# Retention and two feed-forward stages on one core: value weights as the first block row, one product added in PSUM onto a copied bank, and half of the second stage's weights converted during the first

## Chip, cores and metric

The kernel runs on one core of a Trainium2 chip. The metric is device time in microseconds; lower is better. Two figures are used: the time of whole runs (three of the kernel before), and the span of one profiled execution, from its first to its last instruction.

## What is computed

```python
ret = (q @ k.T / sqrt(64)) * Dmat           # causal, Dmat = gamma_h ** (i - j)
x   = (ret @ v), heads side by side         # 2304 tokens x 512
h   = x @ w_in                              # 512 -> 2048
x   = elu(h) @ w_out                        # 2048 -> 512
out = (sigmoid(x @ w_gate) * (x @ w_val)) @ w_o2    # 512 -> 1536 -> 512
```

Inputs are float32; the weights come as pairs of 32-bit words that the kernel converts to float32 itself.

## The kernel before

Every matmul operand is kept as two float32r parts, hi and lo (`split`, lines 105 to 108: ACT casts hi, then POOL or DVE subtracts to get lo), and every product is three matmuls, hi·hi, hi·lo and lo·hi (`mm3`, lines 110 to 114). Every weight tile (128x512) passes through a chain of five stages (`Weight.chain`, lines 137 to 160): stage 1 two ACT instructions (L145, L146), stage 2 two DVE ones (L148, L149), stage 3 one (L152), stage 4 one (L154), stage 5 the split (ACT L107, POOL L108). `load` fetches the raw words by a DMA on SP's queue into one of two buffers.

The order on every engine is the order in which the program is written; nothing reorders it afterwards. The kernel has three parts.

**Retention** (first 125 us): 18 steps, interleaved with pass 0 of the first feed-forward stage.

**First feed-forward stage** (`FF`): 8 passes over d_ff, two blocks `f` of 128 in each; within a pass five token groups `g` (four of 512 tokens, one of 256), so 10 steps per pass. A step makes 12 matmuls up into a bank `h`, ELU (ACT L347, L348, DVE L351), a split into `g`, and two steps later (`LAG`) 12 matmuls down into four `acc` banks; after the second block of a group DVE adds the four banks to `y` (L387). The weights of the next pass, four tiles, are converted in four of the ten steps; `stage()` advances the running chain at four places of a step, and once more at the start of the next.

**Second feed-forward stage**: token groups (0, 1) and then (2, 3) as two `Pair`s, and the last group, 256 tokens, together with pair 0. For the gate and value weights a pair uses Strassen's scheme in Winograd's form: seven half-size `product`s (6 matmuls each) in place of eight, on sums of weights (`Sums`, tile `s`) and on differences of x (`Pair.sum`). There are 12 blocks `f`, each one `unit`: the seven products, sums of them on ACT and DVE, sigmoid and multiplication, splits, and between the products up to five `down`s (6 matmuls each, output tiles of two earlier blocks), placed by `fill(j)`. In pair 0 a unit ends with `single`, 24 matmuls of 256 columns for the last group. In pair 0 `background(f)` converts block f+1's weights `g`, `v`, their sums `s`, and block f's `2`; `bg()` in the unit advances it. The converted tiles are stored to DRAM (`save`) and fetched again for pair 1 (`restore`), both on SP's queue. The first weights of this stage, and the differences of x for pair 0 (`prep`), are made in the last pass of the first stage.

In PSUM the second stage before has four banks that `unit` and `single` take in turn and four for `down`.

Of the kernel before, what the change touches and what calls it, by code (L numbers as in the profile page):

```python
# [47 lines left out]
def retention_elu_glu(  # L48
# [23 lines left out]
    ps_h = ctx.enter_context(tc.tile_pool(name="ps_h", bufs=2, space=bass.MemoryType.PSUM))  # L72

    h_bank = lambda: ps_h.tile([128, 512], F32, tag="h", name="h")

    class Ring:
        def __init__(self, name, pool, n, shape, dtype):
            self.name, self.shape, self.dtype, self.at = name, shape, dtype, 0
            self.homes = [(pool, f"{name}{i}") for i in range(n)]

# [3 lines left out]
        def __call__(self, i=None):  # L84
            if i is None:
                i, self.at = self.at, self.at + 1
            pool, tag = self.homes[i % len(self.homes)]
            return pool.tile(self.shape, self.dtype, tag=tag, name=self.name)
# [4 lines left out]
    w_tile = Ring("w", wpool, 8, [128, 2, DM], F32R)  # L93
    x_tile = lambda g: xpool.tile([128, 2, KB, N[g]], F32R, tag=f"x{g}", name=f"x{g}")
    y_tile = lambda g: ypool.tile([128, KB * N[g]], F32, tag=f"y{g}", name=f"y{g}")

    def u_banks(ps_u):
        at = [0]

        def bank():  # L100
            at[0] += 1
            return h_bank() if at[0] % 2 else ps_u.tile([128, 512], F32, tag="u", name="u")
        return bank
# [25 lines left out]
    class Weight:  # L129
        def __init__(self, src, slot, at=None):  # L130
            self.src, self.slot, self.at, self.w = src, slot, at, None
# [5 lines left out]
        def chain(self, lo_engine=pool):  # L137
# [19 lines left out]
            w = w_tile(self.slot)  # L157
# [6 lines left out]
    for fs in passes:  # L164
        of_pass.append([])
        for f in fs:
            for n, src in (("i", w_in), ("o", w_out)):
                W[n, f] = Weight(src[f], len(weights) % 8)
                weights.append(W[n, f])
                of_pass[-1].append(W[n, f])  # L170


    class Sums:
# [4 lines left out]
        def chain(self):  # L178
            (g0, g1), (v0, v1) = ((t[:, : DM // 2], t[:, DM // 2 :]) for t in (W[n, self.f].f for n in "gv"))
            dve.tensor_tensor(out=v1, in0=v0, in1=v1, op=ALU.add)  # L180
            dve.tensor_tensor(out=v0, in0=g0, in1=v0, op=ALU.subtract)
            yield
            dve.tensor_tensor(out=g0, in0=v1, in1=g0, op=ALU.subtract)
            dve.tensor_tensor(out=g1, in0=g1, in1=g0, op=ALU.subtract)
            yield
            w = s_tile(self.f)
            split(w[:, 0, 0], w[:, 1, 0], W["v", self.f].f, pool)
            split(w[:, 0, 1], w[:, 1, 1], W["g", self.f].f, pool)
            self.w = w
            yield  # L190

    for f in range(FB):
        W["g", f] = Weight(w_gate[f], f % 2 * 3, 0)
        W["v", f] = Weight(w_val[f], f % 2 * 3 + 1, 1)
        W["2", f] = Weight(w_o2[f], (2, 6, 5, 7)[f % 4], 2)
# [196 lines left out]
    class Pair:  # L392
# [23 lines left out]

        def split(self, name, lo_engine):
            p = self.place(name)
            split(p[:, 0], p[:, 1], self.f32(name), lo_engine)
            self.x[name] = p.rearrange("p i (k t) -> p i k t", k=KH)  # L420
# [21 lines left out]
    def unit(pair, f, bg, fill):  # L442

        A, B, D = u_bank(), u_bank(), u_bank()
        s1, s2, s4, sg = (e_tile() for _ in range(4))
        product(1, pair, f, A, True)
        act.copy(s1, A)
        finish_later()
        fill(5)
        bg()  # L450
        product(2, pair, f, B, True)
        dve.tensor_tensor(out=s1, in0=s1, in1=B, op=ALU.add)
        bg()
        fill(0)
# [21 lines left out]
    def glu(g, f, a, b, engine=pool):  # L476
        engine.tensor_tensor(out=a, in0=a, in1=b, op=ALU.mult)  # L477

        def rest():
            n = N[g]  # L480
            if g == 4:
                gt = x_of[3].rearrange("p i k t -> p (i k t)")[:, 2048 + f % 3 * 2 * n : 2048 + (f % 3 + 1) * 2 * n]
                gt = gt.rearrange("p (i t) -> p i t", i=2)
            else:
                gt = g_tile()
            gb[g, f] = gt
            split(gt[:, 0], gt[:, 1], a, pool)
        return rest

    def single(g, f, bg):  # L490
# [3 lines left out]
        hs = []  # L494
        for w in (W["g", f].w, W["v", f].w):
            h = u_bank()[:, :n]
            hs.append(h)
            for k in range(KB):
                c = slice(k * 128, k * 128 + 128)
                mm3(h, w[:, 0, c], w[:, 1, c], x[:, 0, k], x[:, 1, k], k == 0, k == KB - 1)  # L500
            bg()
            if len(hs) == 1:
                act.activation(out=e, in_=h, func=AF.Sigmoid)
        later.append(glu(g, f, e, hs[1], dve))
# [18 lines left out]
    with tc.manual_schedule():  # L523
# [116 lines left out]
        conv = {2: weights[3]}  # L640
        for P in range(len(passes) - 1):
            a, b, ws = begins[P], begins[P + 1], of_pass[P + 1]
            a += 6 * (P == 0) + LAG * (P == 1)
            for i, w in enumerate(ws):
                conv[a + (i * (b - a)) // len(ws)] = w
        a = begins[-2]
# [256 lines left out]
```

## Time and profile before

| | |
|---|---|
| runs | 938.14, 934.47, 936.83 us; median 936.83 us |
| profiled execution | 938.95 us, its span 937.2 us |
| mean granted TensorE clock | 0.987 |
| PE busy | 894.9 us, 95% of the span |
| DVE, ACT, POOL busy | 546.5, 418.2, 408.9 us (58%, 45%, 44%) |

PE's busy time is made of modelled ends: a matmul that follows another at once is shown as overlapping it. What a stretch loses is therefore read from starts of matmuls and their number, and from the waits.

### The profile page before, as it was taken

What the parts mean: (1) busy time and instruction counts of PE and PEld (TensorE: products, weight loads), DVE (VectorE), ACT (ScalarE), POOL (GpSimd) and SP (SyncE); (2) the same over time, 40 slices, a digit from 0 to 9 for tenths busy, and PEclk for the clock granted to TensorE, in tenths of its full rate; (3) what the DMA queues carried; (4) which work ended last, traced back from release to release, by engine and by line L of the source; (5) the groups of instructions that cost most, each with busy time, mean ns of one, the idle gap of its engine ahead of it and who ended that gap; (6) DMA issues with size and microseconds to landing.
All of it is one profiled execution on the core that took longest, in us unless ns stands there. A gap on an engine that the chain in (4) does not pass through costs nothing.

```text
span 937.2 us, 15632 instructions
## 1 busy us (share of the span) xinstructions
PE 894.9 (95%) x6322; PEld 750.1 (80%) x6322; DVE 546.5 (58%) x838; ACT 418.2 (45%) x766; POOL 408.9 (44%) x327
## 2 busy tenths in 40 slices
PE   7899999999999999999988989989999899999997
PEld 5789988888888888888766778777777788888886
DVE  3767635555554645555875878788877732232323
ACT  2345555544545454445554555554544323222221
POOL 1255523333323333333546656665666632323232
PEclk9999999999999999999998999999999999999999
DMA  9646311111111111111034455555455454534232
GB/s 343 204 169 199 98 46 48 66 45 36 33 45 45 45 46 46 46 45 45 23 135 169 169 169 173 200 209 182 171 202 190 157 208 174 202 147 153 105 124 90
DMA packets 43895, 117.18 MB, mean 125 GB/s; under 512 B 8112, under 2 KB 15280, under 8 KB 40752
## 3 DMA queue, kind: packets, MB, share of 16 engines
q1 hardware_dynamic: 42416, 114.70, 35.5%
q10 hardware_dynamic: 1408, 1.49, 0.5%
q8 instruction: 49, 0.80, 0.3%
q14 instruction: 22, 0.18, 0.1%
HBM read 83.15 MB, written 33.03 MB: 124 GB/s over the span
## 4 chain that ended last, share of the span: by engine, by line
PE 67%; DVE 14%; issue 6%; POOL 6%; ACT 5%; DMA 2%; ACTq 0%; POOLq 0%; DVEq 0%; SPq 0%
PE acc L112 10%; PE acc L114 10%; PE acc L113 10%; PE h L113 8%; PE h L112 8%; PE h L114 8%; PE to L241 3%; PE u L112 3%; PE u L113 3%; PE u L114 3%; POOL w L108 2%; DVE t L149 2%; PE h L337 2%; DVE t L152 2%; DVE t L154 2%
## 5 line engine op out<-in xcount | busy, mean ns | idle before, releaser
L108 POOL TENSOR_TENSOR g<-e,g 128x512 fp32r<-128x512 f32 (+1 forms) x134 | 164.4, 1235 | 265.4 <-ACT g L107 209.9
L112 PE MATMUL h<-x,w 128*128 128x512 f32 (+1 forms) x400 | 145.4, 363 | 0.3 <-DVE e L351 0.3
L113 PE MATMUL h<-x,w 128*128 128x512 f32 (+1 forms) x400 | 145.3, 363 | 0.0
L114 PE MATMUL h<-x,w 128*128 128x512 f32 (+1 forms) x400 | 144.8, 362 | 0.0
L351 DVE SCALAR_TENSOR_TENSOR e<-e,h 128x512 f32<-128x512 f32 (+1 forms) x88 | 51.9, 590 | 138.6 <-ACT e L348 138.2
L112 PE MATMUL acc<-g,w 128*128 128x512 f32 (+1 forms) x352 | 124.9, 355 | 4.7 <-DVE y L387 2.4
L477 POOL TENSOR_TENSOR e<-e 128x512 f32<-128x512 f32 x48 | 63.0, 1313 | 142.5 <-ACT e L468 99.9
L114 PE MATMUL acc<-g,w 128*128 128x512 f32 (+1 forms) x352 | 124.6, 354 | 0.3 <-DVE w L108 0.2
L113 PE MATMUL acc<-g,w 128*128 128x512 f32 (+1 forms) x352 | 124.4, 354 | 0.0
L107 ACT CAST g<-e 128x512 fp32r<-128x512 f32 (+1 forms) x136 | 75.3, 571 | 81.2 <-DVE e L351 74.7
L108 POOL TENSOR_TENSOR w<-t,w 128x512 fp32r<-128x512 f32 x65 | 87.6, 1353 | 44.2 <-ACT w L107 44.1
L518 DVE TENSOR_TENSOR y<-y,acc 128x512 f32<-128x512 f32 x90 | 61.0, 684 | 68.4 <-PE acc L114 68.0
L347 ACT ACTIVATE e<-h 128x512 f32<-128x512 f32 (+1 forms) x88 | 45.9, 521 | 115.7 <-PE h L114 101.9
L112 PEld LDWEIGHTS h<-x,w 128*128 128x128 f32 x400 | 75.8, 189 | 13.0 <-DVE e L351 0.7
L113 PEld LDWEIGHTS h<-x,w 128*128 128x128 f32 x400 | 75.7, 189 | 11.9
L114 PEld LDWEIGHTS h<-x,w 128*128 128x128 f32 x400 | 75.6, 189 | 12.0
L387 DVE TENSOR_TENSOR y<-y,acc 128x512 f32<-128x512 f32 (+1 forms) x140 | 79.2, 628 | 0.1
L112 PEld LDWEIGHTS acc<-g,w 128*128 128x128 f32 x352 | 67.0, 190 | 15.0 <-ACT g L107 4.0
L114 PE MATMUL acc<-w,g 128*128 128x512 f32 x192 | 75.7, 394 | 0.8 <-POOL g L108 0.8
L112 PE MATMUL acc<-w,g 128*128 128x512 f32 x192 | 76.0, 396 | 0.0
L113 PE MATMUL acc<-w,g 128*128 128x512 f32 x192 | 76.0, 396 | 0.0
L114 PEld LDWEIGHTS acc<-g,w 128*128 128x128 f32 x352 | 67.1, 190 | 10.1 <-DVE w L108 0.4
(121 smaller groups left out, 1779.8 us busy)
## 6 DMA issues: line engine op xcount, KB each, us to landing
s<-s SPq DMA_DIRECT2D x24, 1024.0 KB, 5.8
in<-in_ain SPq DMA_DIRECT2D x12, 1024.0 KB, 5.7
raw<-in_w_in SPq DMA_DIRECT2D x16, 512.0 KB, 3.5
raw<-in_w_out SPq DMA_DIRECT2D x14, 512.0 KB, 3.5
raw<-in_w_gate SPq DMA_DIRECT2D x12, 512.0 KB, 5.1
raw<-in_w_val SPq DMA_DIRECT2D x12, 512.0 KB, 3.7
raw<-in_w_o SPq DMA_DIRECT2D x12, 512.0 KB, 3.5
g<-w SPq DMA_DIRECT2D x12, 512.0 KB, 5.4
```

The costliest lines, as they stand in the source:

```text
L107: act.copy(hi, src)
L108: lo_engine.tensor_tensor(out=lo, in0=src, in1=hi.bitcast(F32), op=ALU.subtract)
L112: pe.matmul(out_, wh, xh, start=start, stop=False, skip_group_check=shared)
L113: pe.matmul(out_, wh, xl, start=False, stop=False, skip_group_check=shared)
L114: pe.matmul(out_, wl, xh, start=False, stop=stop, skip_group_check=shared)
L149: dve.tensor_scalar(out=u, in0=u, scalar1=5, scalar2=2, op0=ALU.logical_shift_left, op1=ALU.logical_shift_right)
L241: return pe.matmul(out_, w, x, start=start, stop=True, skip_group_check=True)
L347: act.activation(out=e, in_=h, func=AF.Relu, scale=-1.0)
L351: dve.scalar_tensor_tensor(out=e, in0=e, scalar=-1.0, in1=h, op0=ALU.add, op1=ALU.max)
L387: dve.tensor_tensor(out=y[:, e], in0=y[:, e], in1=a, op=ALU.add)
L477: engine.tensor_tensor(out=a, in0=a, in1=b, op=ALU.mult)
L518: dve.tensor_tensor(out=o, in0=o, in1=a, op=ALU.add)
```

## The change

1. **Roles of the weights.** Value weights take the first block row of the Winograd scheme and gate weights the second (`product`: `"vg"` for `"gv"`; `Sums.chain` with g and v exchanged). Value results then come out where the gate results were.
2. **One sum in PSUM.** In `unit` ACT copies the first product, bank A, into a third bank B, where it used to copy it to SBUF; product 2 is added onto B by matmuls that don't start a new sum, so the DVE addition of the two is gone. The order is products 1, 7, 6, 2, 5, 3, 4 (before 1, 2, 7, 6, 5, 3, 4). A single small matmul opens B in the very first unit.
3. **Multiplications.** The sigmoid now works on the two SBUF sums; the two multiplications are on DVE and read the other factor from PSUM (before on POOL, from SBUF).
4. **Banks.** `unit` has five banks in turn, `down` and `single` three; the two halves of `single` share one bank.
5. **Weights of odd blocks** of the second stage (`g`, `v`, `s`, `2` of f = 1, 3, .., 11) are converted in passes 1 to 6 of the first stage, one block in each, into two tiles of the `g` ring that were not used otherwise in that stage (the ring has four tiles there in place of six); they go to DRAM and come back one unit ahead. A pass so converts seven tiles and a `Sums` in eight of its ten steps. In pair 0 `background` has only the even blocks, spread over two units.
6. **Around the border.** `prep` is spread over the last pass one instruction at a time; in that pass only `g`, `v`, `s` of block 0 are converted (before also `g`, `v` of block 1). The two left-over downs of the first stage, the last group's `single` of block 0, and pair 1's differences have other places.

```diff
@@ product, Sums.chain @@
-                w = W["gv"[int(a[0]) - 1], f].w[:, :, at : at + 128]
+                w = W["vg"[int(a[0]) - 1], f].w[:, :, at : at + 128]
@@ unit @@
-        A, B, D = u_bank(), u_bank(), u_bank()
-        s1, s2, s4, sg = (e_tile() for _ in range(4))
+        A, D, B = u_bank(), u_bank(), u_bank()
+        s2, s4 = e_tile(), e_tile()
+        if not u_seen:
+            pe.matmul(B, W["v", f].w[:, 0, :128], pair.x["11"][:, 0, 0], start=True, stop=True, skip_group_check=True)
+        u_seen.append(f)
         product(1, pair, f, A, True)
-        act.copy(s1, A)
+        act.copy(B, A)
         finish_later()
-        fill(5)
+        fill(0)
         bg()
-        product(2, pair, f, B, True)
-        dve.tensor_tensor(out=s1, in0=s1, in1=B, op=ALU.add)
-        bg()
-        fill(0)
         product(7, pair, f, D, True)
         bg()
         product(6, pair, f, A)
         act.copy(s2, A)
-        act.activation(out=s1, in_=s1, func=AF.Sigmoid)
+        fill(1)
         bg()
-        fill(1)
+        product(2, pair, f, B)
+        bg()
         product(5, pair, f, A)
         act.copy(s4, A)
         dve.tensor_tensor(out=s4, in0=s4, in1=D, op=ALU.add)
+        fill(2)
+        act.activation(out=s4, in_=s4, func=AF.Sigmoid)
         bg()
-        fill(2)
         product(3, pair, f, A)
-        act.activation(out=sg, in_=A, func=AF.Sigmoid)
+        dve.tensor_tensor(out=s4, in0=s4, in1=A, op=ALU.mult)
+        bg()
         fill(3)
         product(4, pair, f, D)
-        later.append(glu(pair.g + 1, f, sg, s4))
+        parts(pair.g + 1, f, s4)
         dve.tensor_tensor(out=s2, in0=s2, in1=D, op=ALU.add)
+        bg()
         fill(4)
-        later.append(glu(pair.g, f, s1, s2))
+        act.activation(out=s2, in_=s2, func=AF.Sigmoid)
+        dve.tensor_tensor(out=s2, in0=s2, in1=B, op=ALU.mult)
+        later.append(lambda: parts(pair.g, f, s2))
@@ which step converts what @@
+        for P in range(1, len(passes)):
+            a, f = begins[P], 2 * P - 1
+            if P == len(passes) - 1:
+                items = {0: W["g", 0], 1: W["v", 0], 2: W["s", 0]}
+            else:
+                i0, o0, i1, o1 = of_pass[P + 1]
+                items = {0: i0, 1: W["g", f], 2: o0, 3: W["v", f], 4: W["s", f], 5: i1, 6: W["2", f], 7: o1}
+            for i, w in items.items():
+                conv[a + i + LAG * (P == 1)] = w
@@ prep: one instruction per call of stage() in the last pass @@
+            yield from [()] * (4 * 4)
+            yield from [[i] for i in x("11", pool) + x("21", pool)]
+            yield from [()] * 4
+            yield from [[t("t1")], [t("t3")], *[[i] for i in x("t1", dve)]]
+            h, l = x("t3", pool)
+            yield from [[h], [l, t("t2")], *[[i] for i in x("t2", dve)]]
...
@@ background @@
-            order = "gvgvgvgvgv2s2s2s22" if 0 < f < FB - 1 else "22222" if f else "2s2s2s22"
+            if f % 2 == 0 and f + 2 < FB:
+                names = "gggvgvvv"
...
+            elif f + 1 < FB:
+                names = "2222gvsss2"
@@ loop over units @@
+                    if f and f % 2 == 0:
+                        restore(f + 1, "gvs2")
...
-                at = (1, 2, 3, 4, 2)
+                at = (1, 2, 3, 4, 4) if f else (0, 1, 2, 3, 4)
```

ACT's queue, a whole round of one unit in the middle of pair 0, before: L447, L458, L463 are the copies of bank A after products 1, 6 and 5, L459 and L468 the sigmoids, L503 that of `single`, L107 the casts, L145 and L146 the first stage of a weight's chain.

```order
L503 ACTIVATE e<-h 128x256
L107 CAST w<-t 128x512
L447 COPY e<-h 128x512
L107 CAST g<-e 128x512 x2
L107 CAST x_113<-e 128x256
L145 ACTIVATE t<-raw 128x512
L146 ACTIVATE raw<-raw 128x512
L145 ACTIVATE t<-raw 128x512
L146 ACTIVATE raw<-raw 128x512
L458 COPY e<-h 128x512
L459 ACTIVATE e<-e 128x512
L463 COPY e<-h 128x512
```

The same in the changed kernel, from a unit's first product to its last, odd block: L455 is the copy A to B, L462 and L468 the copies after products 6 and 5, L471 and L482 the sigmoids, L99 the casts, L137 and L138 the first stage of a weight.

```order
L455 COPY u<-u 128x512
L99 CAST g<-e 128x512
L99 CAST x_113<-e 128x256
L137 ACTIVATE t<-raw 128x512
L138 ACTIVATE raw<-raw 128x512
L462 COPY e<-u 128x512
L468 COPY e<-u 128x512
L471 ACTIVATE e<-e 128x512
L99 CAST w<-t 128x512 x2
L99 CAST g<-e 128x512
L482 ACTIVATE e<-e 128x512
```

Between the copy after product 1 and the copy after product 6 there were seven instructions, four of them stage 1 of two weights; now there are five, two of them stage 1 of one weight.

DVE's queue in a pass of the first stage, before: the end of a step with a conversion, a step without one, the start of the next conversion.

```order
L351 SCALAR_TENSOR_TENSOR e<-e,h 128x512
L154 SCALAR_TENSOR_TENSOR t<-raw,t 128x512
L387 TENSOR_TENSOR y_1300<-y_1300,acc 128x512 x4
L351 SCALAR_TENSOR_TENSOR e<-e,h 128x512
L148 TENSOR_SCALAR t<-t 128x512
L149 TENSOR_SCALAR t<-t 128x512
```

The same place in the changed kernel: L140 to L146 are the chain, L348 the ELU, L384 the additions to `y`.

```order
L348 SCALAR_TENSOR_TENSOR e<-e,h 128x512
L146 SCALAR_TENSOR_TENSOR t<-raw,t 128x512
L384 TENSOR_TENSOR y_1300<-y_1300,acc 128x512 x4
L140 TENSOR_SCALAR t<-t 128x512
L141 TENSOR_SCALAR t<-t 128x512
L144 ISA t<-raw,t 128x1024
L348 SCALAR_TENSOR_TENSOR e<-e,h 128x512
L146 SCALAR_TENSOR_TENSOR t<-raw,t 128x512
```

The next conversion now begins right behind the four additions, ahead of the next step's ELU.

## Rows read from the trace of the kernel before

**Rows 1.** Stretches: us, busy us (and instructions) of PE, PEld, DVE, ACT, POOL; clock; DMA.
```profile
476.13:730.23 254.10, 233.13 (x1116) 192.12 (x1117) 198.79 (x281) 132.03 (x239) 157.34 (x115) 0.97 0.51 181
750.00:900.00 150.00, 150.00 (x651) 121.99 (x650) 44.38 (x65) 41.03 (x73) 50.05 (x39) 1.00 0.48 174
122.00:450.00 328.00, 327.65 (x1599) 276.42 (x1600) 177.18 (x301) 164.10 (x293) 113.48 (x95) 1.00 0.14 44
```

**Rows 2.** Matmuls of 256 columns at pair 0's end: start us, us, instruction.
```profile
729.99 0.28 PE L113 MATMUL u<-x,w 128*128 128x256 f32 x1
730.11 0.28 PE L114 MATMUL u<-x,w 128*128 128x256 f32 x1
```

**Rows 3.** PE at the start of pair 1 and near the end, [idle before <-releaser].
```profile
734.14 0.49 PE L112 MATMUL h<-x,s 128*128 128x512 f32 x1 [1.00 <-ACT x L107]
736.72 0.80 PE L113 MATMUL h<-x,s 128*128 128x512 f32 x1 [2.09 <-DVE x L108]
...
923.24 0.49 PE L114 MATMUL acc<-w,g 128*128 128x512 f32 x1 [0.84 <-POOL g L108]
```

**Rows 4.** Whom PE waited for most, 450 to 745 us: total us, times, longest us.
```profile
PE u L112 <- ACT e L458: 9.3, 6, 2.1
PE h L112 <- ACT e L458: 5.4, 4, 1.4
```

**Rows 5.** ACT around one such wait (columns as rows 3).
```profile
628.94 0.67 ACT L145 ACTIVATE t<-raw 128x512 f32<-128x512 f32 x1
...
630.35 0.67 ACT L145 ACTIVATE t<-raw 128x512 f32<-128x512 f32 x1 [0.19 <-DMA raw<-in_w_val]
...
631.67 0.59 ACT L458 COPY e<-u 128x512 f32<-128x512 f32 x1
```

**Rows 6.** PE at the same place: fill's first and last matmul, next product.
```profile
629.35 0.39 PE L112 MATMUL acc<-w,g 128*128 128x512 f32 x1
...
630.49 0.39 PE L114 MATMUL acc<-w,g 128*128 128x512 f32 x1
632.30 0.50 PE L112 MATMUL u<-x,s 128*128 128x512 f32 x1 [1.43 <-ACT e L458]
```

**Rows 7.** One unit of pair 0, from stall to stall (columns as rows 1).
```profile
632.30:653.38 21.08, 19.67 (x96) 16.32 (x97) 17.56 (x26) 10.88 (x21) 13.47 (x11) 1.00 0.54 189
```

**Rows 8.** Pair 1: product 2's first matmul, then ACT's copy of product 1.
```profile
846.06 0.39 PE L112 MATMUL h<-x,w 128*128 128x512 f32 x1
...
846.26 0.59 ACT L447 COPY e<-u 128x512 f32<-128x512 f32 x1 [4.84 <-PE u L114]
```

**Rows 9.** First-stage steps with a conversion: ACT, then DVE (columns as rows 3).
```profile
306.18 0.62 ACT L107 CAST w<-t 128x512 fp32r<-128x512 f32 x1
...
311.01 0.62 ACT L107 CAST g<-e 128x512 fp32r<-128x512 f32 x1 [0.82 <-DVE e L351]
311.54 0.66 ACT L145 ACTIVATE t<-raw 128x512 f32<-128x512 f32 x1
...
304.85 0.69 DVE L351 SCALAR_TENSOR_TENSOR e<-e,h 128x512 f32<-128x512 f32 x1 [1.16 <-ACT e L348]
305.46 0.69 DVE L154 SCALAR_TENSOR_TENSOR t<-raw,t 128x512 uint32<-128x512 uint32 x1
306.06 2.47 DVE L387 TENSOR_TENSOR y<-y,acc 128x512 f32<-128x512 f32 x4
...
312.23 1.07 DVE L148 TENSOR_SCALAR t<-t 128x512 f32<-128x512 f32 x1 [1.25 <-ACT t L145]
...
313.88 0.69 DVE L152 CUSTOM_DVE_ANT_0 t<-raw,t 128x1024 uint16<-128x1024 uint16 x1
```

**Rows 10.** PE: first matmul of the next downs after that evacuation.
```profile
308.67 0.40 PE L112 MATMUL acc<-g,w 128*128 128x512 f32 x1
```

**Rows 11.** L149 on DVE, 125:450 us, then 560:717: busy us, mean ns | idle.
```profile
L149 DVE TENSOR_SCALAR t<-t 128x512 uint32<-128x512 uint32 x26 | 11.1, 427 | 0.9
...
L149 DVE TENSOR_SCALAR t<-t 128x512 uint32<-128x512 uint32 x21 | 23.2, 1103 | 0.7
```

More of the change, by code (lines that the diff above doesn't have):

```diff
@@ L638, in retention_elu_glu @@
                 begins.append(len(ff))
[L640 to L646, printed above, removed]
-        conv.update({a: W["g", 0], a + 2: W["v", 0], a + 4: W["s", 0], a + 6: W["g", 1], a + 8: W["v", 1]})
-        loads = {}
-        for s, w in conv.items():
-            if w not in weights[:4] and isinstance(w, Weight):
-                loads.setdefault(max(0, s - 2), []).append(w)
@@ new lines, in retention_elu_glu, with convert @@
+        raw_order = [conv[s] for s in sorted(conv) if isinstance(conv[s], Weight)]
+        for f in range(0, FB, 2):
+            raw_order += [W[n, f + 2] for n in "gv" if f + 2 < FB] + [W["2", f]]
+        loads = {}
+        for s in range(NSTEP):
+            if s in conv and conv[s] in of_pass[1]:
+                loads.setdefault(s - 2, []).append(conv[s])
+        done = []
+        copies = {}
+        def convert(w, name=None):
+            i = raw_order.index(w) if isinstance(w, Weight) else len(raw_order)
+            for n, _ in enumerate(w.chain()):
+                if n == 3 and 3 <= i < len(raw_order) - 2:
+                    raw_order[i + 2].load()
+                if name and n == (2 if name[0] == "s" else 4):
+                    done.append(name)
+                yield
@@ new lines, in save, with restore @@
+        def save():
+            while done:
+                n, f = done.pop(0)
+                w = W[n, f].w
+                copies[n, f] = dpool.tile(list(w.shape), F32, tag=f"{n}{f}", name=f"{n}{f}")
+                sp.dma_start(out=copies[n, f], in_=w.bitcast(F32))
+        def restore(f, names):
+            for n in names:
+                w = W[n, f].w = s_tile(f % 2) if n == "s" else w_tile(SLOT[n](f))
+                sp.dma_start(out=w.bitcast(F32), in_=copies[n, f])
+        name_of = {id(w): n for n, w in W.items() if n[0] in "gv2s"}
@@ L668, in retention_elu_glu, with ready @@
+        def ready():
+            for work in prep():
+                for i in work:
+                    i()
+                yield
+        halves, prepared = None, ready()
         end = len(ff)
@@ L721, in retention_elu_glu @@
-        done = []
-        def background(f):
-            order = "gvgvgvgvgv2s2s2s22" if 0 < f < FB - 1 else "22222" if f else "2s2s2s22"
-            chains = {n: W[n, f + (n != "2")].chain() for n in set(order)}
-            seen = {n: 0 for n in chains}
-            for n in order:
-                next(chains[n])
-                seen[n] += 1
-                if n != "s" and seen[n] == 4:
-                    at = raws_of.index((n, f + (n != "2"))) + 2
-                    if at < len(raws_of):
-                        W[raws_of[at]].load()
-                if seen[n] == order.count(n):
-                    done.append((n, f + (n != "2")))
-                elif done and n == "2":
-                    save(*done.pop(0))
-                yield
-            while done:
-                save(*done.pop(0))
@@ L820, in retention_elu_glu @@
                 unit(pair, f, bg, fill)
-                if not which:
+                if not which and f:
                     single(4, f, bg)
-                    fill(6)
-                    for _ in work:
-                        pass
+                fill(5)
+                for _ in work:
+                    pass
+                save()
                 if f % 2:
```

211 lines of the change are left out of this document (106 added, 105 removed).

## Prediction

> **What bounds the kernel now.** I read the busy shares by stretch first. In the first feed-forward stage PE is busy without a break (327.65 of 328.00 us) while DVE, ACT and POOL stand at 54, 50 and 35%; in pair 1 PE has 150.00 of 150.00 us; in pair 0, 254.1 us long, it has not, with DVE at 198.79 us, 78%, ACT at 52%, POOL at 62% [rows 1]. So PE is the bound everywhere, and only pair 0 and its borders leave something to gain. How much is read from starts, as PE's ends are modelled. In pair 1 651 matmuls of 512 columns in 150 us are 0.2304 us each [rows 1]; those of 256 columns start 0.12 us apart [rows 2]. Pair 0's stretch has 1116 matmuls [rows 1], by the code 804 of 512 and 312 of 256 columns: 804 x 0.2304 + 312 x 0.12 = 222.7 us. **31.4 us** are lost there. At the start of pair 1, products 1 and 2 from 730.23 on take 12 x 0.2304 us, so product 7 could start at 733.0; it does at 734.14, and its second matmul, instead of 0.23 us later, at 736.72 [rows 3]: 3.5 us, and some 1.5 us (an estimate) for the matmuls that follow at the lower of the clock's two levels. Near the end one matmul waits 0.84 us [rows 3], 1.0 with the overlap that the modelled end hides. Together 31.4 + 5.0 + 1.0 = **37.4 us**.
>
> Next, whom PE waits for in that region: ten waits, 14.7 us, are on L458, ACT's copy of bank A after product 6 [rows 4]; the rest are single. One in close-up: product 6 ends where the fill matmuls begin, at 629.35; ACT is then in stage 1 of two weights, L145 and L146 twice, and comes to the copy at 631.67 [rows 5]; the fill's last matmul starts at 630.49, and product 5, which adds onto A, only at 632.30 [rows 6]. It is ACT's order, not its load: a unit has 10.88 us of ACT work in 21.08. Its 72 x 0.2304 + 24 x 0.12 = 19.5 us of matmuls leave 1.6 us lost [rows 7]. [...]
>
> **The change part by part.** *Matmuls:* one more, 0.2 us; otherwise the same ones in another order. Exchanging value and gate rows costs nothing itself.
>
> *Pair 0's units.* Half of the conversions leave, and ACT has at most one stage 1, two instructions of 0.67 us, between the copies after products 1 and 6. In the order 1, 7, 6, 2, 5 the covers are: copy A to B before product 6, one product, 6 x 0.23 = 1.38 us; copy after 6 before product 5, a fill and a product, 2.76 us (before: a fill). A copy needs 0.20 us from its product's end until ACT starts, 0.59 us [rows 8], and 0.04 until PE goes on [rows 5, 6]: 0.83 us. So 1.38 us leave 0.55 to spare, if ACT is free; ahead stand only sigmoids and casts of the last unit. Were that cover gone, every unit would pay up to 0.8 us. The copy after 6 has ahead of it, from 1.6 us into the unit, copy, two casts and stage 1, about 3.0 us: ACT is ready at 4.6 us, product 6 ends at 4.2, PE wants the bank at 6.9. The copy into PSUM isn't in the trace; the nearest row is the copy out of it, 0.59 us [rows 8]; anything from 0.4 to 1.1 us hides. On DVE each unit loses half of three weights and a `Sums`, 5 us or more, and an addition, and gets two multiplications of some 0.69 us; POOL loses two of 1.3. The multiplication by bank A waits for product 3; behind it on DVE stand a chain's next stage and an addition of a `down`, whose bank comes round only after two more downs. I leave 1 us of waits in the 12 units (0 to 6).
>
> *Storing and fetching,* all on SP. Odd blocks come back in the unit ahead, 2.5 MB in 19.5 us; with saves and raw words some 6.5 MB per two units, 167 GB/s, where pair 0 now has 181 at a DMA share of 0.51 [rows 1]. Pair 1 fetches 2.5 instead of 2.25 MB per unit of 15.2 us, 165 GB/s. In the first stage 44 GB/s become some 125. A save there waits for POOL's split, which is over before L154 of the next step releases the next raw load behind it. No time.
>
> *First stage.* Per pass come three weights and a `Sums`: 10 us on some 27 of 50 for DVE, 75%; ACT and POOL stay below 65 and 50%. But chains now follow step on step, and one is serial. From starts [rows 9]: L154 to cast 0.72, cast to L145 0.53, to L148 0.69, to L152 1.65, to the ELU 0.6 (as L154 to L387), to the next L154 0.61: 4.8 us. With the four additions L387 between: 0.6 + 2.4 + 1.65 + 0.6 + 0.61 = 5.9 us. A step has 24 x 0.2304 = 5.5 us of matmuls, or 4.2 where ups or downs are of 256 columns. The cover: L387 starts at 306.06, its first of four is done 0.69 us later, PE wants that bank at 308.67 [rows 9, 10]: 1.9 us. Passes 2 to 6 have two short steps with chains, 2 x 4.8 - 8.4 = 1.2 us late, covered. Between passes 1 and 2 five chains stand in one full and four short steps: 5.9 + 4.8 + 5.9 + 4.8 + 4.8 - 22.3 = 3.9, less 1.9 = 2.0 us. I take **3 us** lost (0 to 22, rival 1).
>
> *Borders.* In the last pass two of five chains go and the differences come singly, but four of DVE's additions and a lo part of some 1.3 to 2.5 us still meet: 1 us more than what was lost before 476.13 (0 to 4). The first two units have no fills: 0.5. Pair 1's differences start a unit earlier, on a DVE without conversions: of 5.0 us 1 stays. The split of group g+1 at the end no longer stands behind a POOL multiplication: the 1.0 goes.
>
> *Sum.* 1 + 3 + 1 + 0.5 + 1 = 6.5 us stay or come; the gain is 37.4 - 6.5 = **31 us**. On the profiled run, 938.95 us with a span of 937.2 and 1.75 around it, that is 908; this run lies 2.1 above the median, 936.83, which gives 906. I say 906.
>
> [...] L149 takes 0.427 us on average in the first stage, where POOL is busy 35%, and 1.103 in pair 0 with POOL at 62% [rows 1, 11]. [...]
>
> **Rivals.** *1. The first stage gives part back.* L149 is stretched there as in pair 0, by 0.68 us per weight [rows 11]. Steps 0 to 3 of a pass then come 3.5 us late and 5 to 7 another 1.4; less the 1.9 of cover 3 us, for five passes 15, and 7 between passes 1 and 2: 22 in place of 3 us, **925 us**. For it: rows 11. Against: POOL gets to 50% at most, and an instruction that has waited out POOL's leaves the next one clear.
>
> *2. ACT still comes late in pair 0:* stage 1 waits for raw words, or the copy A to B loses its 0.55 us. At 1.3 us for eleven units: **920 us**. For it: L145 waits on a DMA in rows 5. Against: by 0.19 us only.
>
> *3. Slower.* Not L149 alone but all four DVE instructions of a chain are stretched in the first stage. Each 0.1 us per weight beyond 0.68 costs some 42 x 0.1 = 4.2 us over six passes. From about 1.1 us per weight on the whole is slower than now; at twice L149's stretch, 1.36 us, 22 + 29 = 51 us are lost instead of 3: **954 us**. Against: L148, already stretched to 1.07 by a split of POOL's, and L152 and L154 at 0.69 [rows 9] are in the 4.8 us above.
>
> *4. Nothing changes:* the wait moves to the fetched tiles. Odd blocks 5 us late in each of six units lose 30 us: **936 us**. Against: DMA is half idle there.
>
> **Chances.** Forecast 0.63, rival 1 0.15, rival 2 0.12, rival 3 0.05, rival 4 0.05. The forecast's own range is 899 (nothing left over) to 915; to hold 8 in 10 I reach over rival 2 to 921. Faster by over 0.5%, about what a measurement of this kernel can tell from no change: 0.63 + 0.15 + 0.12 = 0.90; within 0.05; slower 0.05.
>
> **What would show it.** [...] Rival 1: waits of `acc` on L384 early in a pass, L141 near 1.1 us. Rival 2: waits on L455 or L462. Rival 4: waits on the DMA of `w` or `s`. The prediction is wrong if the first stage loses over 10 us, or units stay at 21 us.

## The result, and the profile after

| | before | after |
|---|---|---|
| median of 4 runs each | 935.80 us | 907.85 us (906.85 to 908.68) |
| ratio, 95% interval | | 0.970 (0.967 to 0.972) |
| profiled execution, its span | 938.95, 937.2 us | 907.67, 905.9 us |
| mean granted clock | 0.987 | 0.999 |
| DVE, ACT, POOL busy | 546.5, 418.2, 408.9 us | 546.4, 418.1, 338.0 us |

The stretches of [rows 1] in the changed kernel: the same first-stage window, pair 0 from the first matmul of its first unit to the first of pair 1, and a piece of pair 1. Columns as in rows 1.

```profile
122.00:450.00 328.00, 324.02 (x1579) 272.29 (x1578) 248.81 (x396) 196.64 (x353) 158.20 (x125) 1.00 0.39 127
478.89:705.24 226.35, 224.27 (x1118) 188.38 (x1117) 125.92 (x202) 96.85 (x175) 78.16 (x63) 1.00 0.45 164
750.00:890.00 140.00, 140.00 (x607) 113.73 (x606) 48.04 (x72) 39.60 (x67) 24.49 (x19) 1.00 0.40 151
```

Pair 0 takes 226.35 us in place of 254.10: 27.75 less. It begins 2.8 us later, 478.89 against 476.13: that is what the parts ahead of it gave back, taken together. From pair 1's start to the end of the span 937.2 - 730.2 = 207.0 became 905.9 - 705.2 = 200.7: 6.3 less. 27.75 - 2.8 + 6.3 = 31.3 us, the difference of the spans. DVE's busy time is the same; it moved from pair 0 (78% busy before, 56% now) to the first stage (54% before, 76% now).

The 2.8 us have three parts, read by setting the same matmul of both traces side by side: the first 122 us, which the change leaves alone, ran 0.8 us shorter in this execution; the first stage gave back 5.0 us (its 1599 matmuls of [rows 1] take 332.7 us in place of 327.6); the border to pair 0 gained 1.4.

Whom PE waited for from 122 us to the end, all rows of the answer (columns as rows 4):

```profile
PE acc L104 <- ACT w L99: 2.5, 5, 0.8
PE acc L104 <- DVE y L384: 1.7, 2, 1.5
PE u L104 <- ACT u L455: 1.0, 1, 1.0
PE u L104 <- ACT e L462: 0.6, 1, 0.6
PE u L106 <- POOL s L100: 0.5, 1, 0.5
```

The first two rows lie in the first stage (seven waits), the other three between 498 and 513 us, in pair 0's second and third unit. The rows give PE's idle time; read from starts of matmuls a wait is some 0.16 us longer, since a modelled end hides that much, and waits given below "by starts" are counted so. After 513 us PE waits for nobody. In mid pair 0 the waits have turned round: ACT waits for PE, then copies at once. ACT, beginning of one unit (the last column, as in rows 3, is the idle time before and what ended it):

```profile
609.23 0.57 ACT L455 COPY u<-u 128x512 f32<-128x512 f32 x1 [1.00 <-PE u L106]
609.71 0.62 ACT L99 CAST g<-e 128x512 fp32r<-128x512 f32 x1
610.23 0.41 ACT L99 CAST x<-e 128x256 fp32r<-128x256 f32 x1
610.54 0.67 ACT L137 ACTIVATE t<-raw 128x512 f32<-128x512 f32 x1
```

### The profile page after: what moved, and what is told of

Same layout as the page of the kernel before. It is cut to its first block, busy times and chain, and to the rows that moved or that the text cites. A ratio compares the mean times of both kernels' runs of the same rounds, so it can differ in the third digit from the quotient of the medians.

```text
span 905.9 us, 15629 instructions
## 1 busy us (share of the span) xinstructions
PE 880.7 (97%) x6323; PEld 742.4 (82%) x6323; DVE 546.4 (60%) x862; ACT 418.1 (46%) x766; POOL 338.0 (37%) x279
## 4 chain that ended last, share of the span: by engine, by line
PE 68%; DVE 21%; ACT 6%; issue 2%; DMA 1%; POOL 1%; DVEq 0%; ACTq 0%; POOLq 0%; SPq 0%
PE acc L104 10%; PE acc L105 10%; PE acc L106 10%; PE u L104 8%; PE u L106 8%; PE u L105 8%; DVE t L141 4%; DVE y L384 4%; DVE t L144 3%; PE to L238 3%; DVE e L348 3%; PE h L106 3%; PE h L104 3%; PE h L105 3%; DVE t L140 2%; PE h L334 2%
## 5 line engine op out<-in xcount | busy, mean ns | idle before, releaser
L100 POOL TENSOR_TENSOR g<-e,g 128x512 fp32r<-128x512 f32 (+1 forms) x134 | 159.8, 1192 | 436.7 <-ACT g L99 275.9
L99 ACT CAST g<-e 128x512 fp32r<-128x512 f32 (+1 forms) x136 | 77.7, 571 | 126.9 <-DVE e L348 100.3
L105 PE MATMUL h<-x,w 128*128 128x512 f32 (+1 forms) x280 | 103.2, 368 | 0.0
L104 PE MATMUL h<-x,w 128*128 128x512 f32 (+1 forms) x280 | 103.1, 368 | 0.0
L106 PE MATMUL h<-x,w 128*128 128x512 f32 (+1 forms) x280 | 103.0, 368 | 0.0
L348 DVE SCALAR_TENSOR_TENSOR e<-e,h 128x512 f32<-128x512 f32 (+1 forms) x88 | 51.6, 587 | 51.0 <-ACT e L345 50.8
L104 PEld LDWEIGHTS acc<-g,w 128*128 128x128 f32 x352 | 66.5, 189 | 18.1 <-ACT w L99 4.1
L384 DVE TENSOR_TENSOR y<-y,acc 128x512 f32<-128x512 f32 (+1 forms) x140 | 79.1, 628 | 0.0
L100 POOL TENSOR_TENSOR w<-t,w 128x512 fp32r<-128x512 f32 x47 | 63.3, 1350 | 42.5 <-DVE y L523 19.0
L104 PE MATMUL u<-x,s 128*128 128x512 f32 x192 | 76.3, 398 | 1.6 <-ACT u L455 1.0
L106 PE MATMUL u<-x,s 128*128 128x512 f32 x192 | 76.2, 397 | 0.5 <-POOL s L100 0.5
L105 PE MATMUL u<-x,s 128*128 128x512 f32 x192 | 75.8, 395 | 0.0
L106 PEld LDWEIGHTS acc<-g,w 128*128 128x128 f32 x352 | 66.5, 189 | 9.7 <-DVE w L100 0.4
L105 PEld LDWEIGHTS acc<-g,w 128*128 128x128 f32 x352 | 66.6, 189 | 8.7
```

The lines of the kernel that those rows point to most:

```text
L99: act.copy(hi, src)
L100: lo_engine.tensor_tensor(out=lo, in0=src, in1=hi.bitcast(F32), op=ALU.subtract)
L104: pe.matmul(out_, wh, xh, start=start, stop=False, skip_group_check=shared)
L105: pe.matmul(out_, wh, xl, start=False, stop=False, skip_group_check=shared)
L106: pe.matmul(out_, wl, xh, start=False, stop=stop, skip_group_check=shared)
L348: dve.scalar_tensor_tensor(out=e, in0=e, scalar=-1.0, in1=h, op0=ALU.add, op1=ALU.max)
```

## Experiments: the price in the first stage

**left_out** leaves the conversions of the odd blocks out; odd units fetch block 0's tiles in their place.

```diff
-  items = {0: i0, 1: W["g", f], 2: o0, 3: W["v", f], 4: W["s", f], 5: i1, 6: W["2", f], 7: o1}
+  items = {0: i0, 2: o0, 5: i1, 7: o1}
...
-  sp.dma_start(out=w.bitcast(F32), in_=copies[n, f])
+  sp.dma_start(out=w.bitcast(F32), in_=copies[(n, f) if (n, f) in copies else ("s" if n == "s" else "g", 0)])
```

> The changed kernel without the conversions of odd blocks: passes 1 to 6 of the first stage convert only their own four weights, at steps 0, 2, 5 and 7, and odd units fetch copies of block 0's tiles instead, of the same size (so the result is that of other weights). It prices what the moved conversions cost where they went. Theory: the seven waits of 0.4 to 1.6 us in the first stage (5.3 us together) go, all else stays: 902 to 904 us. Rival (these waits come from the order of the additions to y, not from the conversions): 907 to 908.

901.14 us median, ratio to before 0.963 (0.960 to 0.966): 6.7 us below the changed kernel (0.970), somewhat more than expected. Two windows of the first stage, of left_out and then of the changed kernel:

```profile
125.00:450.00 325.00, 325.00 (x1586) 274.95 (x1585) 179.81 (x300) 163.77 (x286) 117.93 (x97) 1.00 0.16 51
```

```profile
125.00:450.00 325.00, 321.02 (x1554) 269.29 (x1553) 248.39 (x395) 194.69 (x348) 156.22 (x124) 1.00 0.39 127
```

PE is again without a break, and six of the seven waits, 4.9 us by starts, are gone; the seventh, 0.4 at the border, stays. The moved conversions cost 6.7 us there for the 27.75 they help to save. The other 1.8 lie in no single wait of the list. Set side by side matmul by matmul, the two traces draw apart by 6.7 us between 178 and 423 us of the changed kernel, nearly all of it at matmuls of downs: 4.9 in the six waits, 0.4 in the six matmuls right behind them, 0.3 at 179 us, and 0.2 each at 238.6, 288.9, 339.1 and 389.4 us, starts too little late to be listed as waits. The rest is in smaller shifts.

## Experiments: which half of the change brings the gain

**moved_only** puts the old unit into the changed kernel; **unit_only** takes the conversions back. Both keep the changed banks and most of the changed border.

```diff
@@ moved_only: unit, product, Sums.chain as before, in the changed kernel @@
+        if f == 2:
+            finish_later()
+        s1, s2, s4, sg = (e_tile() for _ in range(4))
...
+        product(2, pair, f, B, True)
+        dve.tensor_tensor(out=s1, in0=s1, in1=B, op=ALU.add)
...
+        pool.tensor_tensor(out=s1, in0=s1, in1=s2, op=ALU.mult)
@@ unit_only: the changed kernel, conversions in pair 0 @@
-        staged = f % 2
+        staged = 0
...
-                names = "2222gvsss2"
+            names = "22222" if f == FB - 1 else "gvgvgvgvgv2s2s2s22" if f else "2s2s2s22"
...
```

> The changed kernel with the unit of the kernel before: product order 1, 2, 7, 6, 5, 3, 4, sum of products 1 and 2 by DVE in SBUF, multiplications on POOL, roles of gate and value as before. The conversions of odd blocks stay in the first stage, borders and banks as changed. Theory (moving half of the conversions alone takes the two stages 1 apart): the wait on the copy after product 6 falls from 1.4 to 0.1 us or less; first stage 5 us lost as in the changed kernel; 908 to 916 us. Rival (the wider covers of the new product order bring the gain): the copy after product 6 still comes late by some 1 us per unit, 918 to 928.

> The changed kernel with all conversions of the second stage in pair 0 (and the last pass) again, as in the kernel before, each unit 18 stages, g and v alternating; the new unit (product order, sum in PSUM, multiplications on DVE), banks and borders stay. Theory (covers): two stages 1 stand between the copies after products 1 and 6, so ACT is ready at 4.6 + 1.3 = 5.9 us, PE wants the bank at 6.9: no wait there; the first stage loses nothing; DVE has some 18.3 us of work in units of 19.5, 94%, and adds waits of up to 1 us per unit: 903 to 918 us. Rival (DVE or POOL becomes the bound): units of 20.5 us or more, 920 to 935.

moved_only: 924.18 us, ratio 0.988 (0.984 to 0.992). unit_only: 957.28 us, ratio 1.022 (1.018 to 1.026). Both missed the range of their theory. unit_only has the wrong sign: the new unit, alone with all conversions, made the kernel 2% **slower**. moved_only's time lies where its rival put it, but not for the rival's reason, a copy that comes late by some 1 us in each unit. moved_only gives 12 of the 28 us, unit_only loses 21; the two together give more than their sum. In moved_only most of the wait of each unit does go, but the copy after product 6 still costs 4.7 us in six waits, and one wait of 5.2 us by starts stands at unit 2, where the first copy was held by POOL's split of an earlier unit, a cause that comes up again below:

```profile
521.31 0.59 ACT L454 COPY e<-u 128x512 f32<-128x512 f32 x1 [3.67 <-POOL g L100]
```

Whom PE waited for in unit_only's pair 0:

```profile
PE u L104 <- ACT u L455: 19.8, 11, 3.6
PE u L104 <- ACT e L462: 16.5, 9, 3.2
```

Twice per unit ACT is late: with the copy A to B, and with the copy after product 6. ACT around both in one unit:

```profile
656.61 0.62 ACT L99 CAST w<-t 128x512 fp32r<-128x512 f32 x1 [1.99 <-DVE t L146]
657.14 0.58 ACT L455 COPY u<-u 128x512 f32<-128x512 f32 x1
...
662.53 0.66 ACT L137 ACTIVATE t<-raw 128x512 f32<-128x512 f32 x1 [2.82 <-DMA raw<-in_w_val]
...
663.66 0.56 ACT L462 COPY e<-u 128x512 f32<-128x512 f32 x1
```

ACT isn't busy: it stands still 1.99 us before a cast whose input DVE hasn't made (L146 began at 655.13 and took 1.45 us), and 2.82 us before a stage 1 whose raw words haven't landed (their DMA was issued at 656.61, right behind that L146, which frees the buffer). The copies behind inherit both waits. This is rival 2's mechanism, in full.

**unit_early** is unit_only with the stages moved away from there.

```diff
-                step = stepper(work, 8 + (0 if which or not f else 2) + len(ours), count)
+                step = stepper(work, 5 + (0 if which or not f else 2) + len(ours), count)
```

> unit_only (the changed kernel with all conversions in pair 0) with the 18 stages of a unit spread over its first twelve calls in place of fifteen, so that the chain of block f's third weight ends, and the next raw words are asked for, some 4 us ahead of the unit's end. Theory (unit_only lost 2.0 us twice per unit since the last cast, which waits for DVE, stands ahead of the copy A to B, and since stage 1 of v, which waits for its raw words, stands ahead of the copy after product 6; places, not load): at least one of the two waits goes, 915 to 938 us, and if both go about 908. Rival (the load of pair 0 with the new unit is too high wherever the stages stand): 945 to 960 us.

924.75 us, ratio 0.988 (0.984 to 0.991): of the 49 us that unit_only lies above the changed kernel 32 were a matter of places, not of load; the other 17 were not taken apart. The time is as expected, but neither wait is gone: they shrink to 9.9 and 6.4 us in all (L462, L455). The raw words are still late, by 1.66 us at 644.24 and 1.75 at 665.94; the unit between these two waits takes 21.71 us.

## Experiments: is it ACT's order alone?

The prediction read the wait on L458 as ACT's order: two stages 1 ahead of a copy [rows 5]. If that is all, the kernel before can be mended in one line.

**one_at_a_time.**

```diff
-            order = "gvgvgvgvgv2s2s2s22" if 0 < f < FB - 1 else "22222" if f else "2s2s2s22"
+            order = "gggggvvvvv2s2s2s22" if 0 < f < FB - 1 else "22222" if f else "2s2s2s22"
```

> The kernel before with one line changed: the background of a unit of pair 0 runs the chain of g to its end, then that of v, instead of alternating them. Load, places of the conversions, products and banks stay. Theory (it is ACT's order): one stage 1 of 1.33 us is left between the copies after products 1 and 6, so the ten waits on that copy (14.7 us) shrink to 0 to 0.4 us each; but the stage 1 of v now stands ahead of the copy after product 5, which can be up to 0.7 us late in some units. 916 to 926 us against 936. Rival (it is the load of pair 0, 78% on DVE, and only work that leaves helps): waits move to another place, 932 to 938.

947.76 us, ratio 1.013 (1.010 to 1.016): slower, a clear miss. The wait on L458 didn't shrink:

```profile
PE u L112 <- ACT e L458: 12.9, 6, 5.0
PE h L112 <- ACT e L458: 7.5, 5, 1.5
```

One of the eleven, at 507 us, is 5.0 us long, behind a cast that waits 3.77 us for DVE; the others are about as long as before. New are seven waits of 0.5 to 0.66 us for L503, the sigmoid of `single`. ACT at the place of [rows 5], one unit:

```profile
655.74 0.66 ACT L146 ACTIVATE raw<-raw 128x512 int32<-128x512 uint32 x1
657.90 0.59 ACT L458 COPY e<-h 128x512 f32<-128x512 f32 x1 [1.50 <-POOL g L108]
```

Now ACT is free at 656.40, as planned, and still doesn't copy: it waits for POOL. POOL there, and then POOL of the kernel before around [rows 5]:

```profile
655.17 2.69 POOL L108 TENSOR_TENSOR g<-e,g 128x512 fp32r<-128x512 f32 x2
```

```profile
628.92 2.72 POOL L108 TENSOR_TENSOR g<-e,g 128x512 fp32r<-128x512 f32 x2
```

The copy writes tile s2. The `e` ring has six tiles, a unit with its `single` takes five, so s2 is the tile that was s1 in the unit before it, and POOL's split still reads it, until 628.92 + 2.72 = 631.64 in the kernel before. ACT's stages 1 ended at 631.6 (rows 5: 630.35, two instructions), the copy began at 631.67. Two waits ended there within 0.1 us of each other, and the trace names one. The next two runs take POOL's away, without and with ACT's.

**tiles_order** and **tiles_and_one_at_a_time.**

```diff
@@ both @@
-        s1, s2, s4, sg = (e_tile() for _ in range(4))
+        s1, sg, s4, s2 = (e_tile() for _ in range(4))
@@ tiles_and_one_at_a_time: also the line of one_at_a_time @@
```

> The kernel before with one line changed: the four e tiles of a unit are taken in the order s1, sg, s4, s2 instead of s1, s2, s4, sg, so that the copy after product 6 (into s2) no longer gets the tile that POOL's split of the last unit's s1 still reads (in the ring of six, the second tile of a unit is the first of the unit ahead). ACT's order stays. Theory (two waits end there almost together, ACT's two stages 1 and POOL's split, 631.58 and 631.64 in the trace of before): taking POOL's away alone changes nothing, 933 to 938 us. Rival (POOL's split was the only cause): the ten waits of 1.4 us go, 918 to 924 us.

> Both: the kernel before with one chain after another (as in one_at_a_time) and the e tiles in the order s1, sg, s4, s2. Theory (two causes, each sufficient): the 1.66 us per unit on the copy after product 6 go, the 0.7 us per unit behind the sigmoid of the last group's single stay: 948 - 10 x 1.6 = 932, so 927 to 936 us. Rival (POOL's split doesn't matter): 944 to 950 us, as one_at_a_time.

tiles_order: 935.93 us, ratio 1.000 (0.998 to 1.002), as expected: with POOL's wait gone ACT's order still holds the copy, and eleven waits on L458, 11.6 us, are left. tiles_and_one_at_a_time: 946.22 us, ratio 1.011 (1.007 to 1.015), a miss in time, though the copy does what was expected. ACT, one unit:

```profile
636.24 0.66 ACT L146 ACTIVATE raw<-raw 128x512 int32<-128x512 uint32 x1
636.80 0.57 ACT L458 COPY e<-u 128x512 f32<-128x512 f32 x1
...
640.58 0.62 ACT L107 CAST w<-t 128x512 fp32r<-128x512 f32 x1 [2.67 <-DVE t L154]
641.11 0.66 ACT L145 ACTIVATE t<-raw 128x512 f32<-128x512 f32 x1
641.67 0.66 ACT L146 ACTIVATE raw<-raw 128x512 int32<-128x512 uint32 x1
642.22 0.57 ACT L463 COPY e<-u 128x512 f32<-128x512 f32 x1
```

L458 follows stage 1 at once: for this copy both causes are shown, each sufficient by itself. Only two waits on it are left of eleven, the long one of 5.0 us (at 508 us) and one of 0.84. But the second stage 1 now stands, behind a cast that waits 2.67 us for DVE, ahead of the next copy, L463, and PE waits there and for the sigmoid of `single` instead:

```profile
PE u L112 <- ACT e L458: 5.9, 2, 5.0
PE h L112 <- ACT e L463: 5.5, 6, 1.0
PE u L112 <- ACT e L463: 4.8, 5, 1.1
PE u L112 <- ACT e L503: 3.9, 4, 1.0
```

**moved_tiles** is moved_only with that tile order, and with the split of the last group's block 0 inside unit 1; in moved_only it stood ahead of unit 2's first copy, where the 5.2 us were lost. The diff is against moved_only.

```diff
-        if f == 2:
-            finish_later()
-        s1, s2, s4, sg = (e_tile() for _ in range(4))
+        if not pair.g:
+            e_tile.at = 5 * f
+        s1, sg, s4, s2 = (e_tile() for _ in range(4))
...
+            (0, 1, 3): [finish_later],
```

> moved_only (the changed kernel with the old unit) with the e tiles in the order s1, sg, s4, s2, and the split of the last group's block 0 inside unit 1 instead of ahead of unit 2's first copy, which had cost 5.2 us and a stretch at the lower clock there. Theory (moving takes ACT's cause away, the tile order POOL's): waits on the copy after product 6 go altogether, 5.2 + 3.3 us at unit 2 and four of 0.65 us go: 924 - 11 = 913, so 910 to 916 us. Rival (something else of the new unit is needed in the middle of pair 0): units keep 0.6 us waits, 915 to 919 us.

914.56 us, ratio 0.977 (0.973 to 0.981), as expected. Moving the conversions, freeing s2's tile and placing that split earlier, with the old order of products, the DVE sum and POOL's multiplications, bring some 21 of the 28 us. Of the rest, 2.6 us sit at pair 0's start (5.2 us of waits by starts against 2.6), 2.5 in three single waits at the end of pair 0 and of the kernel, and some 1.5 in the matmuls behind the longest wait, 0.09 us late each from 503.1 to 506.3 us; nothing in mid pair 0, where no wait is left in either.

**sum_in_sbuf** takes away the part that gives the change its name, the sum in PSUM.

```diff
-        act.copy(B, A)
+        act.copy(s1, A)
...
-        product(2, pair, f, B)
+        product(2, pair, f, B, True)
+        dve.tensor_tensor(out=s1, in0=s1, in1=B, op=ALU.add)
...
-        dve.tensor_tensor(out=s2, in0=s2, in1=B, op=ALU.mult)
+        dve.tensor_tensor(out=s2, in0=s2, in1=s1, op=ALU.mult)
```

> The changed kernel without its sum in PSUM: ACT copies bank A after product 1 to SBUF, product 2 starts a sum of its own in bank B, DVE adds the two (0.69 us per unit) and the last multiplication reads that sum from SBUF; the order of products, banks, conversions and all else stay. Theory (what the new unit brings is its order, two fewer e tiles and POOL's relief; the sum in PSUM only saves an addition on a DVE that is at 53 to 57% in pair 0): 906 to 910 us. Rival (the sum in PSUM is needed, since B's DVE addition makes a bank or tile come late): 912 to 920 us.

907.34 us, ratio 0.969 (0.967 to 0.971), against 0.970 (0.967 to 0.972) of the changed kernel. The sum in PSUM by itself brings nothing that can be measured here.

## Experiments: the wait of each pass in the first stage

In each of passes 2 to 6 PE stands still 0.6 to 0.95 us by starts, once. DVE, POOL and ACT, then PE, around one of them in the changed kernel:

```profile
316.39 1.49 POOL L100 TENSOR_TENSOR g<-t,g 128x512 fp32r<-128x512 f32 x1
...
316.75 1.41 DVE L141 TENSOR_SCALAR t<-t 128x512 uint32<-128x512 uint32 x1
...
318.90 0.68 DVE L348 SCALAR_TENSOR_TENSOR e<-e,h 128x512 f32<-128x512 f32 x1
...
319.49 0.69 DVE L146 SCALAR_TENSOR_TENSOR t<-raw,t 128x512 uint32<-128x512 uint32 x1
...
320.10 2.48 DVE L384 TENSOR_TENSOR y<-y,acc 128x512 f32<-128x512 f32 x4
...
320.92 0.47 PE L104 MATMUL acc<-g,w 128*128 128x512 f32 x1 [0.43 <-ACT w L99]
```

Step 7's chain, with L141 drawn out to 1.41 us beside POOL's split (0.43 us at 312.51, with no split beside it), makes the ELU (L348) late, so the additions to `y` begin at 320.10; the first of the four, 0.68 us long, ends at 320.78. Step 8 has ups of 256 columns, from 318.89, which cover 12 x 0.12 = 1.44 us. The trace names ACT's cast, which ended last, but these matmuls read weights converted a pass earlier; it is the bank that is late. The matmul starts 0.14 us after the first addition's end, as at 188.39 us (0.15), where the trace names L384. Two runs separate the parts.

**lo_by_act** and **step_later.**

```diff
@@ lo_by_act: Weight.chain @@
-            split(w[:, 0, :], w[:, 1, :], f, lo_engine)
+            if self.home is g_tile:
+                act.copy(w[:, 0, :], f)
+                act.copy(w[:, 1, :], f)
+            else:
+                split(w[:, 0, :], w[:, 1, :], f, lo_engine)
@@ step_later @@
-                conv[a + i + LAG * (P == 1)] = w
+                conv[a + i + (2 if P == 1 else i == 7)] = w
```

> The changed kernel with the lo parts of the odd blocks' tiles g, v and 2, in the first stage, written by ACT as a copy in place of POOL's subtraction (18 of them, 0.62 us on ACT for 1.3 to 1.5 us on POOL; the lo parts so hold other values). Theory (L141 takes 1071 ns there on average since it waits out POOL's split that runs beside it, and this makes the ELU of step 7 late, so that step 8, with 1.44 us of ups as cover, stalls 0.6 us): L141 after these splits falls to 0.43 us, its mean over the first stage to 0.7 to 0.85; the stalls of 0.6 us shrink to under 0.2 in passes 2 to 6, 903.5 to 906 us. Rival (the stretch is not POOL's doing, or the stall comes from the order of the queue alone): L141 stays above 0.95 us and the time within 1 us of 907.9.

> The changed kernel with the last of a pass's eight conversions in passes 2 to 6 (w_out of the next pass's second block) at step 8 instead of 7. Theory (the stall of each pass is step 7's chain, which puts the four additions to y late, ahead of step 8, whose ups of 256 columns cover only 1.44 us): the five stalls of 0.6 to 0.95 us go, 3.3 us: 904 to 905.5 us. Rival (the stall follows the chain, wherever it stands): 907 to 909 us.

lo_by_act: 903.15 us, ratio 0.964 (0.962 to 0.967), a little below what was expected; step_later: 904.70 us, ratio 0.966 (0.964 to 0.968), as expected. In both all five waits are gone. L140 and L141 over 125 to 450 us, of the changed kernel and of lo_by_act (columns as rows 11):

```profile
L141 DVE TENSOR_SCALAR t<-t 128x512 uint32<-128x512 uint32 x44 | 47.1, 1071 | 1.5
...
L140 DVE TENSOR_SCALAR t<-t 128x512 f32<-128x512 f32 x44 | 26.2, 596 | 31.9 <-ACT t L137 31.8
```

```profile
L141 DVE TENSOR_SCALAR t<-t 128x512 uint32<-128x512 uint32 x44 | 37.3, 849 | 1.5
...
L140 DVE TENSOR_SCALAR t<-t 128x512 f32<-128x512 f32 x44 | 24.6, 559 | 37.4 <-ACT t L137 37.3
```

With 18 of POOL's splits gone L141 falls by 0.22 us on average; 849 ns is the upper end of what was expected. POOL's splits of the activations stay. In step_later the last chain stands in step 8, and step 7's additions follow the ELU at once (DVE):

```profile
316.83 0.69 DVE L348 SCALAR_TENSOR_TENSOR e<-e,h 128x512 f32<-128x512 f32 x1 [2.74 <-ACT e L345]
317.44 2.47 DVE L384 TENSOR_TENSOR y<-y,acc 128x512 f32<-128x512 f32 x4
```

So the wait needs both: a chain made late by POOL, and a step with a short cover behind it.

**step_later_and_borders**, a version that beats both kernels.

```diff
-                conv[a + i + LAG * (P == 1)] = w
+                conv[a + (i + 2 if P == 1 else (1, 2, 3, 4, 5, 6, 8, 9)[i] if P == 2 else i + (i == 7))] = w
-                names = "2222gvsss2"
+                names = "2222gvsss2" if f > 1 else "22gvsss222"
-            (0, 1, 0): [x_last],
-            (0, 1, 2): [lambda: single(4, 0, nothing)],
+            (0, 0, 4): [x_last],
+            (0, 1, 1): [lambda: single(4, 0, nothing)],
```

> step_later, and: in pass 2 the conversions one step later still (steps 1 to 6, 8, 9), which leaves one step free behind pass 1's; in the first two units the last group's x is cast a place later in unit 0 and its block 0 a place earlier in unit 1, and the sums s of block 2 are made two stages earlier in unit 1. Theory: besides the 3.3 us, up to 1.6 us between passes 1 and 2, 0.8 behind the cast of x at 498 us and 1.8 around s at 510 us go: 900.5 to 903 us. Rival (what is moved makes the next one late): 903 to 906 us.

902.07 us (900.84 to 902.49), ratio 0.963 (0.961 to 0.965), as expected, 5.8 us below the changed kernel, within 1 us of left_out, which does without six blocks' conversions. All waits that are left after 122 us:

```profile
PE acc L104 <- DVE y L384: 1.0, 2, 0.8
PE u L104 <- ACT e L468: 0.7, 1, 0.7
PE u L104 <- ACT u L455: 0.6, 1, 0.6
```

## Why the prediction was right, and where it was not

The forecast was 906 us, measured were 907.85; by the profiled executions, 31 us of gain forecast and 31.3 found. The mechanism came as forecast in the main: PE's waits in the middle of pair 0 go and units take 19.5 us, for a smaller loss in the first stage; the granted clock over pair 0 was 0.97 and is 1.00. That the sum is met within half a us is partly luck, since its terms are off by up to 2.4 us and cancel: 1.9 in pair 0 and 2.0 in the first stage one way, 2.4 at the border, 1.3 in pair 1 and 0.8 in the first 122 us the other. The terms:

- **Pair 0, 31.4 us lost before.** By the same counting 805 x 0.2304 + 312 x 0.12 = 222.9 us of matmuls now stand in 226.35: 3.4 are left, where I had 1 in the units and 0.5 in the first two. In the units there is no wait after 513 us, so the 1 was too much; at the start the step "the first two units have no fills: 0.5" was too small: three waits of 2.6 us together, behind the cast of the last group's x (498 us) and the sums s of block 2 (510 and 513 us).
- **ACT's order.** The step "It is ACT's order, not its load" was half of it. POOL's split held the same copy to within 0.1 us, by way of the tile ring, and one_at_a_time shows that mending ACT's order alone gives nothing. The gain came as forecast since the change takes both away: fewer stages 1 on ACT, and two `e` tiles a unit in place of four. My covers (0.83 of 1.38 us, 4.6 against 6.9) held in the changed kernel, but they rest on the moved conversions, which unit_only shows.
- **First stage, 3 us, and border, 1 us.** Pair 0 begins 2.8 us later, where 4 were forecast, but the parts differ. The first stage gave back 5.0 us, not 3, and its 1599 matmuls take 332.7 us, 327.6 before. Between passes 1 and 2 the wait is 1.6 us by starts, 2.0 forecast. Passes 2 to 6 were to cost nothing: 0.6 each, 0.95 in the last. The step that failed is the cover: I took 1.9 us, that of a step with full ups, for "two short steps ... 1.2 us late, covered". Step 8 has short ups, 1.3 us less; 1.9 - 1.3 = 0.6, and 1.2 - 0.6 leaves the 0.6 that was found. At the border 0.4 us is left of what was lost before, where I added 1: it gained 1.4.
- **Pair 1's start and the end.** 5 of 6 us forecast, 6.3 found; the 1 that I left there wasn't needed.
- **Rival 1** was right on its sign and wrong on its price: L141 does take 1.07 us in the first stage. But L140 fell from 0.83 (as L148) to 0.60, and the pair, 0.83 + 0.43 = 1.26 us before, is 1.67 now, as long as the 1.65 from L148 to L152 that my serial loop already held. From 125 to 450 us each of the 29 L141 that began while a split of POOL's ran ended 0.28 to 0.29 us after it, and the other 15 took 0.43 us; lo_by_act agrees (1071 to 849 ns on average when 18 of POOL's splits go). That an instruction which has waited out POOL's leaves the next one clear held in the first stage before, where all 26 L149 took 0.43 us, but not after: the L140 at 316.22 us ended 0.29 us after one split, and the L141 behind it, in the rows above, ran beside the next. What such a stretch costs here is set by the cover behind it: 0.6 us a pass, and nothing with the chain one step on.
- **Rivals 2 to 4.** Rival 2 didn't come, but unit_only shows that it was near: with all conversions it costs 957 us. No wait on a fetched tile appears (rival 4), and the first stage's loss stays far from rival 3's; there my working gives break-even at 0.68 + 0.1 x 11 / 4.2 = 0.94 us per weight, not 1.1.

## What to carry to other kernels

Before a wait is put down to an engine's order, look at what else ended at the same moment on the tile that the waiting instruction writes: here a ring one tile short held the same copy, and taking either cause away alone gave nothing or less than nothing. Where an engine takes its instructions in the order of the program, as ACT does here, a background stage's own wait, for raw words or for another engine's result, falls on whatever urgent copy stands behind it (1.99 and 2.82 us in one unit of unit_only); such stages belong where nothing urgent follows, or in another stage of the program with a cover that is counted in its shortest step. And two edits that each lose, or half gain, alone can be worth making together.

## What the runs showed of the hardware

- DVE's two instructions of stage 2, from 125 to 450 us: one that began while a split of POOL's ran ended 0.28 to 0.29 us after that split. Before, these were 18 of the 26 L148, and the other 8 took 0.42 us, all L149 0.43; after, 38 of the 44 L140 and 29 of the 44 L141, and the others took 0.42 to 0.43. So the delay is shared differently from place to place: before, the first took 834 ns on average and the second 427; after, 596 and 1071. In the rows of 316 us above it is L141 that runs beside POOL's split, 1.41 us. The first of them in the kernel before, 125 to 450 us (the second is in rows 11):

```profile
L148 DVE TENSOR_SCALAR t<-t 128x512 f32<-128x512 f32 x26 | 21.7, 834 | 12.6 <-ACT t L145 12.5
```

- Behind a wait of about 2 us matmuls sometimes start farther apart for a stretch and sometimes not; why was not followed. In the kernel before, behind the wait of 2.09 us at the start of pair 1, the granted clock was 0.50 from 737.31 to 739.45 us, and matmuls of 512 columns started 0.43 us apart; from 739.85 us on it was 1.00, and they started 0.23 us apart. The seven that start from 736.72 us on take 3.13 us in place of 7 x 0.2304 = 1.61, the prediction's 1.5 us. In unit_only, after a wait of 1.79 us, they start 0.43 us apart; after one of 2.07 us, 0.23 us apart but for the first:

```profile
567.47 0.62 PE L104 MATMUL u<-x,s 128*128 128x512 f32 x1 [1.79 <-ACT e L462]
567.89 0.63 PE L105 MATMUL u<-x,s 128*128 128x512 f32 x1
568.32 0.63 PE L106 MATMUL u<-x,s 128*128 128x512 f32 x1
```

```profile
664.27 0.50 PE L104 MATMUL u<-x,s 128*128 128x512 f32 x1 [2.07 <-ACT e L462]
664.60 0.39 PE L105 MATMUL u<-x,s 128*128 128x512 f32 x1
664.83 0.39 PE L106 MATMUL u<-x,s 128*128 128x512 f32 x1
```
